# An attention and mixture kernel on one core: the transfers that stack q and k in another order, and the left queries' sums between the heads

## The chip, the cores and the metric

The kernel runs on one core of one Trainium2 chip. The metric is the device time of one execution in microseconds (us), taken as the median of several runs. The profile is one further execution, recorded by the hardware profiler.

## The reference

Inputs are fp32: q, k and v of 4 batches x 8 heads x 576 tokens x 64, and the weights of two feed-forward stages. What is computed:

```python
q_rot, k_rot = rotate(q), rotate(k)                  # rotary embedding
scores = (q_rot @ k_rot.T) / sqrt(64)
attn = exp(scores - rowmax);  attn = attn / (rowsum + 1e-9)
x = (attn @ v), heads side by side                   # 2304 x 512
x = (sigmoid(x @ w_gate) * (x @ w_val)) @ w_out      # hidden width 1536
h = x @ w_in                                         # hidden width 1024
solu = h * softmax(h);  ln = (solu - mean) / sqrt(var + 1e-6) * g
out = ln @ w_out2
```

## The kernel before, in words

The program has three stages one after the other: attention (about the first 300 us of the span), the gated stage with `gate_val` and `out_part`, and the last stage with the layer norm. The diff touches only attention, and of that only SyncE's transfers and the columns that the softmax's sums are written to.

**Pairs and steps.** Attention works through 16 pairs of heads (`pairs`). A pair has 9 groups of queries (`order`): four of 128 queries for head 0, one that holds the 64 left queries of both heads (tokens 512 to 575), four for head 1. A loop over `g` runs through 16 x 9 steps. At step g the kernel issues, in order: the row maximum of group g on VectorE (`row_max`, L376), the evacuations left over from the step before, the exponential on ScalarE with its row sums (`exps`, L381), the score matmuls of group g + 1 (`scores`, L369), and then what an agenda holds for this step (`advance`). The agenda is filled from the table `SLOTS`: for the pair that begins at step 9i, an entry `name=n` puts that work at step 9i + n. Within a step, entries of the kind REST run in the order in which the pairs registered them, a lower pair first.

**How q and k get to TensorE.** For a coming pair, GpSimd turns q and k (`turn`, at steps -16 and -15), TensorE transposes them in three parts (`qk_bank`, L303 and L306, at -11, -9 and -8), ScalarE and VectorE write a rounded part and a rest (L431, L434) into a tile of the pair, `st0`. As 4 blocks of 576 columns, its `flat` view holds: rounded k (0), rounded q (1), rest of k (2), rest of q (3); head 0 in partitions 0 to 63, head 1 in 64 to 127. `D` is 64, `P` is 128. For the scores the rounded part and the rest of one head must lie one above the other in 128 partitions, so `stack` (at -6) copies inside on-chip memory with five transfers from SyncE's queue. Three build the tile `st1` of head 1 (L315 to L317). Two then overwrite head 1's half of `st0` with head 0's parts (L318, L319); they must wait until the transfers that read the bytes to be overwritten have landed. The first scores of the pair, issued at step -1, read `st0`: the first matmul of them reads blocks 0 and 1 (written last by L318), the second reads blocks 1 and 2 (block 2 written by L319).

**The sums.** `exps` writes the sum of group n into one column of a 128 x 9 tile; `sum_at` puts the left queries' column last. `weigh` adds 1e-9 and takes the reciprocal (at 11), `weigh_t` transposes the nine columns on TensorE (13), `weigh_out` stores them as one run of 9 x 128 values in DRAM (14, L408), and `spread` (21, L416) broadcasts them back over partitions as the tile `wt` with four transfers: head 0 main, head 1 main, head 0 left, head 1 left. `scale_x` multiplies the output with it on GpSimd at step 24 (L426).

**SyncE's queue.** All these transfers are issued in program order from one queue, and one that waits holds up those behind it. Since 9(i - 3) + 21 = 9i - 6, the spread of pair i - 3 stands directly ahead of the stack of pair i. Behind it come, one step on, the loads of q and k of a later pair (`load_qk`, L211 and L215), `weigh_out` and the two `join` transfers (`um`, L487).

The tile framework puts in the waits itself, from the regions that each instruction reads and writes.

Of the kernel before, what the change touches and what calls it, by code (L numbers as in the profile page):

```python
# [20 lines left out]
def kernel(  # L21
# [21 lines left out]
    nc = tc.nc  # L43
    B, H, S, D = q.shape
# [3 lines left out]
    P = 128  # L48
    MAIN, LEFT, HALF = 512, 64, 288
# [155 lines left out]
    def load_qk(i, t=None):  # L205

        b, hp = pairs[i]
        hs = slice(2 * hp, 2 * hp + 2)
        raws[i] = t = raw_p.tile([P, 2, NSL, D], F32, tag="raw", name=f"raw{i}") if t is None else t
        for j, src in enumerate((k, q)):  # L210
            yield nc.sync.dma_start(  # L211
                out=t[:, :, 4 * j:4 * j + 4, :], in_=src[b, hs, 0:MAIN, :].rearrange("h (p r) d -> p h r d", r=4)
            )
        for j, src in enumerate((k, q)):
            yield nc.sync.dma_start(  # L215
                out=t[j * LEFT:(j + 1) * LEFT, :, 8, :], in_=src[b, hs, MAIN:S, :].rearrange("h t d -> t h d")
            )
# [90 lines left out]
            src = ps[:, 0:P].rearrange("p (a t) -> p a t", a=2)  # L308
        return [(h_out, l_out, src)]

    def stack(i):
        s0, s1 = stacks[i, 0].bitcast(F32), stacks[i, 1].bitcast(F32)
        flat = s0.rearrange("p a b s -> p (a b) s")
        dma = nc.sync.dma_start
        dma(out=s1[D:P], in_=flat[D:P, 0:3])  # L315
        dma(out=s1[0:D, 0:2], in_=flat[D:P, 2:4])
        dma(out=s1[0:D, 2], in_=flat[D:P, 0])  # L317
        dma(out=flat[D:P, 0:2], in_=flat[0:D, 2:4])  # L318
        dma(out=flat[D:P, 2], in_=flat[0:D, 0])  # L319

    def stack_first(h, step):

# [23 lines left out]

    order = [(0, 0), (0, 1), (0, 2), (0, 3), None, (1, 0), (1, 1), (1, 2), (1, 3)]
    NTL = len(order)
    sum_at = [0, 1, 2, 3, 8, 4, 5, 6, 7]
    e_tiles = {}  # L350
    sums = {}
    wts = {}
# [26 lines left out]
    def exps(i, n, ps, nm):  # L379
        e = e_p.tile([P, S], F32, tag="e", name=f"e{i}_{n}")  # L380
        nc.scalar.activation(  # L381
            out=e.rearrange("p (j c) -> p j c", j=2),
            in_=ps[:, :, :HALF],
            func=AF.Exp,
            bias=nm,
            accum_out=sums[i][:, sum_at[n]:sum_at[n] + 1],
        )
        e_tiles[i, n] = e

# [21 lines left out]
    def spread(i):  # L411
        d = wts[i]
        w = wt_p.tile([P, S], F32, tag="wt", name=f"wt{i}")
        for c0, n, at in ((0, MAIN, 0), (MAIN, LEFT, 2 * MAIN)):
            for h in range(2):
                nc.sync.dma_start(  # L416
                    out=w[h * D:(h + 1) * D, c0:c0 + n],
                    in_=d[at + h * n:at + (h + 1) * n].unsqueeze(0).to_broadcast([D, n]),
                )
        wts[i] = w  # L420

    def scale_x(i):
# [104 lines left out]
    FIRST, GROUP, ATTEND, REST = "first", "group", "attend", "rest"  # L527
    agenda = {}

    def at(g, kind, fn, *args):  # L530
        agenda.setdefault((g, kind), []).append((fn, args))


    SLOTS = dict(
        te=(1, 3, 4, 5, 6, 7, 8, 9, 11),
        corner=8,
        left=(6, 11),
        av=(((6, 2), (8, 9)), ((9, 4), (10, 9)), ((11, 2), (12, 6), (13, 9)), ((14, 9),)),
        join=(18, 19),
        add=(20, 24),  # L540
        weigh=11,
        weigh_t=13,
# [2 lines left out]
        scale=24,  # L545
        turn=(-16, -16, -15, -15),
        bank=(-11, -9, -8),
        stack=-6,
        split_v=-1,
        stack_left=0,  # L550
        load_qk=-23,
# [4 lines left out]
        sum_eng=0,  # L556
        uw=(1, 0, 0, 0),
        bank1=(1, 1, 1),
        stack1=3,
        first_b=(-1, -1, 2),  # L560
        turn1=(0, 0, 0, 0),
        split_v0=0,
# [29 lines left out]
    for i in range(NPR):  # L592
        g = i * NTL
        own = SLOTS_FIRST if i == 0 else SLOTS_LAST if i == NPR - 1 else SLOTS
        for n in range(NTL):
            at(g + own["te"][n], FIRST, transpose_e, i, n)
        at(g + own["corner"], GROUP, transpose_corner, i)
        for h in range(2):
            at(g + own["left"][h], GROUP, transpose_left, i, h)
            for j in range(2):  # L600
                m0 = 0
                for slot, m1 in own["av"][2 * h + j]:
                    at(g + slot, ATTEND, attend, i, h, j, m0, m1)
                    m0 = m1
            at(g + own["join"][h], REST, join, i, h)
            at(g + own["add"][h], REST, add, i, h)
        for name, fn in (
            ("weigh", weigh), ("weigh_t", weigh_t), ("weigh_out", weigh_out), ("spread", spread), ("scale", scale_x)
        ):
            at(g + own[name], REST, fn, i)  # L610

        if i > 1:
            at(max(0, g + SLOTS["load_qk"]), REST, lambda i: [None for _ in load_qk(i)], i)
            at(max(0, g + SLOTS["load_v"]), REST, load_v, i)
            for m, slot in enumerate(SLOTS["turn"]):
                at(max(0, g + slot), REST, turn, i, m)
        if i > 0:
            for part, slot in enumerate(SLOTS["bank"] if i > 1 else [b - NTL for b in SLOTS["bank1"]]):
                at(g + slot, GROUP, qk_bank, i, part)
            at(g + (SLOTS["stack"] if i > 1 else SLOTS["stack1"] - NTL), REST, stack, i)  # L620
            at(g + SLOTS["split_v"], REST, split_v, i)
            at(g + SLOTS["stack_left"], REST, stack_left, i)
    cur, late, moved = [], [], []
# [24 lines left out]
    for u in range(3):  # L648
        g = (W_PAIR + 2 * u) * NTL
# [36 lines left out]
    if True:  # L686
# [32 lines left out]
        for g in range(NPR * NTL):  # L719
            i, n = divmod(g, NTL)  # L720
            if g == (NPR - 1) * NTL:
                prep_ctx.close()
                xs_pool["p"] = x_ctx.enter_context(tc.tile_pool(name="xs", bufs=XS, side="right", reuse_waits="tile"))
            if g == 1:
                et = et_p.tile([P, 2, 2, 4, S], F32R, tag="et", name="et")
            nm = row_max(i, n, sc)
            if SLOTS["exp_pos"] == 0:
                exps(i, n, sc, nm)
            evacuate_h(cur)
            if SLOTS["exp_pos"] == 1:  # L730
                exps(i, n, sc, nm)
            evacuate_h(late)
            if SLOTS["exp_pos"] == 2:
                exps(i, n, sc, nm)
            evacuate_u()
            if SLOTS["exp_pos"] == 3:
                exps(i, n, sc, nm)
            evacuate_l()
            if g + 1 < NPR * NTL:
                sc = scores(*divmod(g + 1, NTL))  # L740
            advance(g)
# [381 lines left out]
```

## Time and profile before

| | |
|---|---|
| median of 3 runs | 967.11 us (964.16 to 969.16) |
| the profiled execution: its own time | 964.83 us |
| its span, first to last instruction | 963.1 us |
| mean granted TensorE clock | 0.995 of full |
| busy over the span: PE, PEld, DVE | 923.1 us, 801.5 us, 647.7 us |
| busy over the span: ACT, POOL | 501.7 us, 444.0 us |

PE is TensorE's matmuls, PEld its weight loads (which overlap matmuls), DVE is VectorE, ACT ScalarE, POOL GpSimd, SP SyncE. SPq is SyncE's queue of transfers. The shares over the whole span mix three stages with different limits; what attention is bound by has to be read from its own stretch.

### The profile page before, as it was taken

The numbers are of one execution on the slowest core, as the hardware profiler recorded it, in microseconds if no ns is written. First come the engines' busy times: TensorE is split into PE (matmuls) and PEld (weight loads), VectorE is DVE, ScalarE is ACT, GpSimd is POOL, SyncE is SP. The second block draws the span as 40 slices with busy tenths as digits, with TensorE's granted clock in tenths as the row PEclk, the third lists the DMA queues.
The fourth block names the chain that finished last, engine by engine and source line by source line (L and its number), as shares of the span: only waits on it lengthen the run. The fifth ranks groups of instructions, "written<-read, shape, count | busy, mean of one in ns | idle before, by whom it ended". The sixth has DMA issues, their size and how long they took to land.

```text
span 963.1 us, 14429 instructions
## 1 busy us (share of the span) xinstructions
PE 923.1 (96%) x5128; PEld 801.5 (83%) x5128; DVE 647.7 (67%) x1073; ACT 501.7 (52%) x994; POOL 444.0 (46%) x356
## 2 busy tenths in 40 slices
PE   4999999899999899999999999999999989999998
PEld 3889889899898688898788898788898768888886
DVE  7999989999888955346345355545456787666661
ACT  4888989898987323133111123112123576666662
POOL 5668879889845533344324344324343531111110
PEclk9999999999999999999999999999999999999999
DMA  3666677676754310103101012100112334334332
GB/s 108 141 169 165 152 191 180 160 188 159 160 141 122 104 66 22 44 23 94 38 22 44 23 45 88 44 22 22 44 46 71 103 64 90 66 72 93 66 77 44
DMA packets 92311, 86.10 MB, mean 89 GB/s; under 512 B 52608, under 2 KB 77456, under 8 KB 92240
## 3 DMA queue, kind: packets, MB, share of 16 engines
q1 hardware_dynamic: 92240, 85.19, 35.7%
q8 instruction: 40, 0.66, 0.3%
q14 instruction: 31, 0.25, 0.1%
HBM read 46.83 MB, written 4.79 MB: 54 GB/s over the span
## 4 chain that ended last, share of the span: by engine, by line
PE 63%; DVE 14%; DMA 10%; POOL 4%; issue 4%; ACT 2%; SPq 2%; DVEq 0%; POOLq 0%; ACTq 0%
DMA st<-st 9%; PE gv L680 9%; PE gv L681 9%; PE gv L679 9%; PE y L790 4%; PE y L789 4%; PE y L788 4%; PE po L977 3%; PE po L976 3%; PE po L978 3%; PE ph L881 3%; PE ph L882 3%; PE ph L883 3%; DVE nm L376 3%; DVE et L434 2%
## 5 line engine op out<-in xcount | busy, mean ns | idle before, releaser
L774 POOL TENSOR_TENSOR gs<-g,gs 128x512 fp32r<-128x512 f32 (+1 forms) x59 | 74.1, 1257 | 261.2 <-DVE gs L773 203.9
L769 ACT ACTIVATE sg<-gv 128x512 f32<-128x512 f32 (+1 forms) x60 | 33.3, 555 | 288.2 <-PE gv L681 288.2
L679 PE MATMUL gv<-xs,w 128*128 128x512 f32 (+1 forms) x480 | 177.4, 370 | 2.1 <-ACT w L137 2.1
L681 PE MATMUL gv<-xs,w 128*128 128x512 f32 (+1 forms) x480 | 177.5, 370 | 1.2 <-POOL w L138 1.2
L680 PE MATMUL gv<-xs,w 128*128 128x512 f32 (+1 forms) x480 | 177.4, 370 | 1.0 <-DVE xs L514 1.0
L771 DVE TENSOR_TENSOR g<-gv,sg 128x512 f32<-128x512 f32 (+1 forms) x60 | 38.2, 636 | 174.5 <-ACT sg L769 164.9
L381 ACT ACTIVATE e<-s,nm 128x576 f32<-128x576 f32 x144 | 107.3, 745 | 16.9 <-DVE nm L376 16.4
L369 PE MATMUL s<-st 128*128 128x288 f32 x512 | 102.8, 319 | 13.8 <-DMA st<-st 7.0
L376 DVE TENSOR_REDUCE nm<-s 128x1 f32<-128x576 f32 x144 | 107.2, 745 | 5.5 <-PE s L369 4.0
L681 PEld LDWEIGHTS gv<-xs,w 128*128 128x128 f32 x480 | 90.9, 189 | 17.3 <-POOL w L138 2.1
L680 PEld LDWEIGHTS gv<-xs,w 128*128 128x128 f32 x480 | 90.5, 189 | 17.5 <-DVE xs L514 2.7
L679 PEld LDWEIGHTS gv<-xs,w 128*128 128x128 f32 x480 | 90.5, 188 | 17.4 <-ACT w L137 2.5
L434 DVE TENSOR_TENSOR et<-te,et 128x512 fp32r<-128x512 f32 x144 | 98.3, 684 | 9.7 <-ACT et L431 8.5
L481 PE MATMUL av<-et,vs 128*128 128x288 f32 x512 | 99.9, 316 | 0.3 <-DVE uw L632 0.3
L369 PEld LDWEIGHTS s<-st 128*128 128x128 f32 x512 | 75.3, 193 | 23.2 <-DMA st<-st 6.3
L790 PE MATMUL y<-gs,w 128*128 128x512 f32 (+1 forms) x240 | 88.3, 368 | 0.0
L789 PE MATMUL y<-gs,w 128*128 128x512 f32 (+1 forms) x240 | 88.2, 368 | 0.0
L788 PE MATMUL y<-gs,w 128*128 128x512 f32 (+1 forms) x240 | 88.2, 367 | 0.0
L440 PE MATMUL te<-ident,e 128*128 128x128 f32 x576 | 87.0, 274 | 0.7 <-DVE et L434 0.7
L431 ACT CAST et<-te 128x512 fp32r<-128x512 f32 x144 | 84.2, 586 | 5.3 <-PE te L440 5.2
L481 PEld LDWEIGHTS av<-et,vs 128*128 128x128 f32 x512 | 73.0, 189 | 1.6 <-DVE uw L632 1.0
L440 PEld LDWEIGHTS te<-ident,e 128*128 128x128 f32 x576 | 71.1, 141 | 1.1 <-DVE et L434 0.9
(128 smaller groups left out, 1958.1 us busy)
## 6 DMA issues: line engine op xcount, KB each, us to landing
wraw<-in_moe_w_out_dram SPq DMA_DIRECT2D x20, 512.0 KB, 4.6
st<-st SPq DMA_DIRECT2D x30, 288.0 KB, 3.1
st<-st SPq DMA_DIRECT2D x15, 432.0 KB, 4.0
wraw<-in_moe_w_gate_dram SPq DMA_DIRECT2D x12, 512.0 KB, 4.0
wraw<-in_moe_w_val_dram SPq DMA_DIRECT2D x12, 512.0 KB, 4.5
um<-uw SPq DMA_DIRECT2D x32, 144.0 KB, 2.4
st<-st SPq DMA_DIRECT2D x30, 144.0 KB, 4.9
rawv<-in_v_dram SPq DMA_DIRECT2D x16, 256.0 KB
```

The source lines that it names most:

```text
L369: nc.tensor.matmul(ps[:, j, :HALF], w, x, start=m == 0, stop=m == len(mm) - 1)
L376: nc.vector.tensor_reduce(out=nm, in_=ps[:, :, :HALF], axis=AX.XY, op=ALU.max, negate=True)
L381: nc.scalar.activation(out=e.rearrange("p (j c) -> p j c", j=2), in_=ps[:, :, :HALF], func=AF.Exp, bias=nm, accum_out=sums[i][:, sum_at[n] ...
L434: nc.vector.tensor_sub(out=l_out, in0=ps, in1=h_out.bitcast(F32))
L440: nc.tensor.transpose(ps[:, r * P:(r + 1) * P], e[:, r * P:(r + 1) * P], ident)
L481: nc.tensor.matmul(av[:, :HALF], *mm[m], start=m == 0, stop=m == len(mm) - 1)
L679: nc.tensor.matmul(ps[:, :n], wh, x[:, 0, :n], start=kk == 0, stop=False)
L680: nc.tensor.matmul(ps[:, :n], wh, x[:, 1, :n], start=False, stop=False)
L681: nc.tensor.matmul(ps[:, :n], wl, x[:, 0, :n], start=False, stop=kk == KD - 1)
L788: nc.tensor.matmul(ys[m][:, :n], wh, g[:, 0, :n], start=first, stop=False)
L789: nc.tensor.matmul(ys[m][:, :n], wl, g[:, 0, :n], start=False, stop=False)
L790: nc.tensor.matmul(ys[m][:, :n], wh, g[:, 1, :n], start=False, stop=last)
```

## The change

`stack` is cut into two steps. Step 0 issues the four transfers that read head 1's half: the one that copied three blocks is cut into one of two blocks and one of one block, and the two that read the blocks which the first overwriting transfer needs now come first. Step 1 issues the two that overwrite. Both steps stand in the same slot (-6, and 3 for pair 1), one directly behind the other, so that six transfers stand where five stood. The sums go out in the order of the groups (the left queries' row between the heads, as row 4), and `spread` needs three transfers instead of four: head 0 whole, head 1 main, head 1 left.

```diff
-    def stack(i):
+    def stack(i, step):
+
         s0, s1 = stacks[i, 0].bitcast(F32), stacks[i, 1].bitcast(F32)
         flat = s0.rearrange("p a b s -> p (a b) s")
         dma = nc.sync.dma_start
-        dma(out=s1[D:P], in_=flat[D:P, 0:3])
-        dma(out=s1[0:D, 0:2], in_=flat[D:P, 2:4])
-        dma(out=s1[0:D, 2], in_=flat[D:P, 0])
-        dma(out=flat[D:P, 0:2], in_=flat[0:D, 2:4])
-        dma(out=flat[D:P, 2], in_=flat[0:D, 0])
+        if step == 0:
+            dma(out=s1[D:P, 0:2], in_=flat[D:P, 0:2])
+            dma(out=s1[0:D, 2], in_=flat[D:P, 0])
+            dma(out=s1[0:D, 0:2], in_=flat[D:P, 2:4])
+            dma(out=s1[D:P, 2], in_=flat[D:P, 2])
+        else:
+            dma(out=flat[D:P, 0:2], in_=flat[0:D, 2:4])
+            dma(out=flat[D:P, 2], in_=flat[0:D, 0])
...
-    sum_at = [0, 1, 2, 3, 8, 4, 5, 6, 7]
...
-            accum_out=sums[i][:, sum_at[n]:sum_at[n] + 1],
+            accum_out=sums[i][:, n:n + 1],
...
-        for c0, n, at in ((0, MAIN, 0), (MAIN, LEFT, 2 * MAIN)):
-            for h in range(2):
-                nc.sync.dma_start(
-                    out=w[h * D:(h + 1) * D, c0:c0 + n],
-                    in_=d[at + h * n:at + (h + 1) * n].unsqueeze(0).to_broadcast([D, n]),
-                )
+
+        for h, c0, n, at in ((0, 0, S, 0), (1, 0, MAIN, S + LEFT), (1, MAIN, LEFT, S)):
+            nc.sync.dma_start(
+                out=w[h * D:(h + 1) * D, c0:c0 + n], in_=d[at:at + n].unsqueeze(0).to_broadcast([D, n])
+            )
...
-        stack=-6,
+        stack=(-6, -6),
...
-        stack1=3,
+        stack1=(3, 3),
...
-            at(g + (SLOTS["stack"] if i > 1 else SLOTS["stack1"] - NTL), REST, stack, i)
+            for step, slot in enumerate(SLOTS["stack"] if i > 1 else [s - NTL for s in SLOTS["stack1"]]):
+                at(g + slot, REST, stack, i, step)
```

## Rows read from the trace of the kernel before

**Rows 1.** The page, busy us of the whole span, share and instructions.
```profile
PE 923.1 (96%) x5128; PEld 801.5 (83%) x5128; DVE 647.7 (67%) x1073; ACT 501.7 (52%) x994; POOL 444.0 (46%) x356
```
**Rows 2.** The page, the chain that ended last: shares of the span by line.
```profile
DMA st<-st 9%; PE gv L680 9%; PE gv L681 9%; PE gv L679 9%; PE y L790 4%; PE y L789 4%; PE y L788 4%; PE po L977 3%; PE po L976 3%; PE po L978 3%; PE ph L881 3%; PE ph L882 3%; PE ph L883 3%; DVE nm L376 3%; DVE et L434 2%
```
**Rows 3.** Windows of one pair each: stretch, length, busy us (x instructions) by engine.
```profile
core 0: us, PE busy (x) PEld busy (x) DVE busy (x) ACT busy (x) POOL busy (x), PEclk, DMA share, GB/s
50.60:68.19 17.59, 16.81 (x131) 16.11 (x132) 16.17 (x28) 15.84 (x38) 13.19 (x10) 1.00 0.65 156
68.19:85.55 17.36, 16.79 (x131) 16.06 (x131) 15.65 (x28) 15.39 (x38) 14.59 (x11) 1.00 0.71 169
85.55:102.52 16.97, 16.76 (x131) 16.11 (x131) 15.45 (x27) 15.10 (x37) 14.55 (x11) 1.00 0.70 166
102.52:120.84 18.32, 16.82 (x132) 16.11 (x132) 17.18 (x30) 16.80 (x41) 14.52 (x11) 1.00 0.66 155
...
156.53:174.74 18.21, 16.80 (x131) 16.08 (x131) 16.88 (x30) 17.22 (x42) 14.94 (x11) 1.00 0.76 192
...
192.30:210.11 17.81, 17.22 (x133) 16.09 (x131) 17.36 (x30) 17.09 (x42) 15.47 (x12) 1.00 0.79 189
...
sum 229.26, PE 218.38 PEld 208.67 DVE 211.92 ACT 204.97 POOL 186.77; mean PE 16.80 PEld 16.05 DVE 16.30 ACT 15.77 POOL 14.37
```
**Rows 4.** PE's waits, 30 to 300 us: total us, times, longest us.
```profile
PE s L369 <- DMA st<-st: 7.0, 16, 1.1
```
**Rows 5.** PE's timeline: start, us, instruction [idle before it and what ended it].
```profile
67.45 0.37 PE L369 MATMUL s<-st 128*128 128x288 f32 x1 [0.41 <-ACT et L431]
138.16 0.37 PE L369 MATMUL s<-st 128*128 128x288 f32 x1 [0.86 <-ACT st L431]
191.70 0.63 PE L303 MATMUL tq<-ident,turned 128*128 128x128 f32 x4 [1.03 <-DVE et L434]
209.43 0.37 PE L369 MATMUL s<-st 128*128 128x288 f32 x1 [0.26 <-ACT et L431]
227.09 0.63 PE L303 MATMUL tq<-ident,turned 128*128 128x128 f32 x4 [1.05 <-DVE et L434]
```
**Rows 6.** SyncE's queue over one stack: start and duration of each issue.
```profile
161.57 2.46 SPq L416 DMA_DIRECT2D wt<-d  x4
164.13 0.54 SPq L315 DMA_DIRECT2D st<-st  x1
164.72 0.59 SPq L316 DMA_DIRECT2D st<-st  x1
165.35 1.60 SPq L317 DMA_DIRECT2D st<-st  x1
170.77 0.46 SPq L318 DMA_DIRECT2D st<-st  x1
171.33 0.54 SPq L319 DMA_DIRECT2D st<-st  x1
```
**Rows 7.** The chain over the same stack: start, us, what.
```profile
165.35 5.40 DMA st<-st
...
171.33 3.37 DMA st<-st
...
174.74 0.67 PE s L369 x3
```
**Rows 8.** Line L318, its 14 transfers: issue to landing.
```profile
DMA to landing us min/median/max: 3.1/3.1/3.1
```
**Rows 9.** Line L317, its 14 transfers: issue to landing.
```profile
DMA to landing us min/median/max: 4.9/5.6/6.2
```
**Rows 10.** The page, transfers: count, KB each, median us to landing.
```profile
st<-st SPq DMA_DIRECT2D x15, 432.0 KB, 4.0
...
um<-uw SPq DMA_DIRECT2D x32, 144.0 KB, 2.4
```
**Rows 11.** DVE's waits, 30 to 300 us.
```profile
DVE et L434 <- ACT et L431: 6.1, 22, 0.5
```

## The prediction

> **What bounds the kernel now.** I first read the page. TensorE's matmuls fill 96% of the span [rows 1], so time comes back only where PE stands idle, or where its work shrinks; the change takes no work from PE. The chain that ended last gives 9% of the span to one kind of transfer, `st<-st` [rows 2], which is `stack`. That share is no price: it says that the chain runs through those transfers, not how long anyone waited for them. So I cut attention into windows of one pair, each ending where the second of a pair's score matmuls could go [rows 3]. In 13 pairs (229.26 us) PE is idle 229.26 - 218.38 = 10.9 us. The reader is to see what is left of a pair when PE's idle time is taken off: 17.59 - 0.78, 17.36 - 0.57, 16.97 - 0.21, 18.32 - 1.50, 18.21 - 1.41 leave 16.81, 16.79, 16.76, 16.82 and 16.80. The idle time differs by a factor of seven and the rest is constant. PE makes up nothing of what it lost, so a stall of PE here costs its full length.
>
> Then who causes the stalls. The list of PE's waits names the stack's landing 16 times, 7.0 us [rows 4]. Three more waits of a pair's first score matmul, 0.41 + 0.86 + 0.26 = 1.53 us, are put down to ScalarE [rows 5]; the matmul behind each of them waits for the stack again, and I count these to the stack too: 8.5 us in 11 pairs, 0.78 us for each pair that waits. Nearly all of the rest is two waits of 1.03 and 1.05 us for the transposes of the next pair (L303) [rows 5], which the change doesn't touch. Pair 1 stacks five steps before its first scores are issued and has nothing to gain.
>
> Last, SyncE's queue over one stack [rows 6]. The three transfers that build `st1` are issued at 164.13, 164.72 and 165.35; L318, which overwrites, goes only at 170.77, right where the third landed (165.35 + 5.40 [rows 7]). L319 follows at 171.33 and lands 3.37 later, at 174.70; PE goes on at 174.74 [rows 7]. So the path is: first issue, 6.6 us until the third has landed, 0.6 us to L319's issue, 3.4 us to its landing: 10.6 us. From 170.75 until L318 starts nothing of the stack is in flight.
>
> **The change, part by part.**
>
> *The overwriting transfers.* Now the first of them needs only the first two reads, 288 and 144 KB, which is just the size and order of L318 and L319. That pair lands 3.1 [rows 8] and 0.56 + 3.37 = 3.9 us after the first issue [rows 6, 7]. So the first overwriting transfer goes 3.9 us after the stack's start instead of 6.6, while the other two reads are still in flight, and stands behind their bytes. The bytes of the four reads are the same 864 KB, so I let them land where the three did, 6.6 us after the start. Behind them 144 KB more take 0.83 us (L318 lands at 170.77 + 3.1 = 173.87, L319 at 174.70), so 288 KB take about 1.6 and the first overwriting transfer lands at 8.2, against 6.6 + 3.1 = 9.7 before: 1.5 us earlier. The second waits for the other two reads, goes at 6.7, and lands behind the first at 8.2 + 0.8 = 9.0, or at the 2.4 us that 144 KB take alone [rows 10], 6.7 + 2.4 = 9.1; against 10.6 that is 1.5 earlier. I take 1.4. Bounds: nothing, if the first overwriting transfer is made to wait for all four reads; 2.7 us if the stream's bytes cost it nothing (6.6 - 3.9). Against the first bound speaks that L319 doesn't wait for L318, though both write one tile, and that a pair's first matmul goes before L319 has landed [rows 5, 7]: waits go by region.
>
> *One more issue.* The cut transfer adds an issue of 0.46 to 1.60 us on SyncE [rows 6]; the third in a row takes 1.60 and may hand that wait to the fourth. I take 0.6 and price it at nothing, because SyncE waits from about 3 to 3.9 and up to 6.6 us anyway; if that cover were gone it would cost 0.6 us of the 1.4. How late three reads land varies from 4.9 to 6.2 us [rows 9], and moves both orders alike.
>
> *Spread.* Four issues take 2.46 us and the stack's first issue stands 0.1 us behind them [rows 6]; three take 0.6 less. Where the stack's source is written earlier than that, its start moves by up to 0.6 us; where it waits for VectorE, by nothing. I take 0.2 for a mean. The sum on SyncE is neutral past the stack (six for five, three for four), and what stands behind (loads of q and k, `weigh_out`, the joins) is free about as much sooner as the start moves. `scale_x` reads `wt` three steps later, so the larger single transfer stays hidden; exposed it would cost some tenths of a microsecond on GpSimd, which is busy 14.4 of 17.6 us [rows 3].
>
> *The sums' columns.* The same activations write to other columns: nothing, either way. `weigh` waits for all nine as before.
>
> *What the landing is worth.* Landing 1.4 to 1.6 us sooner covers waits of 0.21 to 1.50 us [rows 3], so at most 8.5 us go. What is late next is VectorE: it is busy 17.18, 16.88 and 17.36 us in three pairs that hold weight decoding [rows 3], and it loses 6.1 us in some 15 pairs, 0.4 a pair, waiting for ScalarE's half of an evacuation [rows 11]. With that these pairs can't go below 17.6, 17.3 and 17.8, which leaves 0.7, 0.9 and 0 us to gain in place of 1.5, 1.4 and 0.6: 1.9 us given up. Shorter pairs also bring the first scores some 0.3 us closer to the stack; in the three longest waits that leaves about 0.3 us each, 0.9 in all. Sum: 8.5 - 1.9 - 0.9 = 5.7, and I take 6 us.
>
> One rule speaks against the cut: the Trainium skill, "DMA: Bandwidth & Descriptors", section "Rules for kernel authors", says to coalesce many small transfers into one large one, and that transfers to separate partition halves run one after the other. By it, the two pieces of the cut transfer cost more than the whole. The row says that a 144 KB transfer behind one of 288 KB adds 0.83 us, the rate of its bytes and no more [rows 6, 7, 8]; by the row the cut costs nothing in the stream. What the rule would make of the time is the second rival.
>
> A second rule concerns the stalls: "Trainium Kernel Development and Optimization" of the Trainium skill, section "Best Practices", has distance from the limit judged by weight loads rather than by matmul busy time. PEld is busy 16.05 us a pair and PE 16.80 [rows 3]; by the rule PE could catch up 0.75 us a pair, and then most stalls would already be absorbed and the sum would be near nil. The constant rest of 16.8 us is the measurement against it.
>
> **The rivals.**
>
> 1. *The stalls turn into other waits.* VectorE is busy 16.3 us of 17.6 on the mean, ScalarE 15.8 [rows 3], each in strict order; freed of the stack, PE may wait for row maxima, evacuations or the transposes of the next pair. For it: the 1.03 and 1.05 us waits for L303 are there already [rows 5]. Against it: the pair that waited only 0.21 us took 16.97 us, so the other engines can do such a pair; but that pair held no decoding. If only the pairs without decoding gain (about 0.78 + 0.57 + 0.21 and 0.4 for the pair before them, some 2 us) the time is 965. The case in which the framework holds the first overwriting transfer for all four reads comes out alike: 0.2 us a pair from the spread, 11 x 0.2 = 2 us. Both: no change that a measurement tells.
> 2. *The extra transfer costs a transfer's own time (slower).* If the fourth read ran after the third instead of in its stream, it would land 2.4 us later [rows 10], and the second overwriting transfer, which needs it, with it: 2.4 - 1.4 = 1.0 us later than before, on 11 pairs that already wait, 11 us: 978. It decides from an added 1.4 us on. The 0.83 us of [rows 6 to 8] speaks against it. The Trainium skill's rule on small transfers, above, points this way.
> 3. *All of it comes off.* No engine takes the place of the stack: 8.5 us, 958, with the spread's share helping in the longest pairs. For it speaks the constant rest of a pair; against it VectorE's 17.2 and 17.4 us.
>
> **How the numbers follow.** The forecast (a part of the stalls goes, 4 to 7.5 us) has 0.6, the first rival 0.2, the second 0.05, the third 0.15. The sum is made against the profiled execution's own 964.83 us (its span and 1.7 us around it): 964.8 - 6 = 959. That execution lies 2.3 us under the median of the runs, 967.1; from the median it would be 961. The mean of the four executions shown is 966.3, so I say 960.5. The range must take in the full 8.5 us from the profiled time, 956, and nearly the whole first rival counted from the median, 965.5. A measurement of this kernel tells about 0.5% from no change, 4.8 us. Most of the forecast and all of the third rival lie beyond that, allowing for the runs' own spread: faster 0.63; within it the first rival and the small end of the forecast: 0.31; slower, the second rival: 0.06.
>
> **What would show it.** In the profile after: the first overwriting issue about 4 us after the stack's first, before the third and fourth reads have landed; the second at 6.6 to 6.8, landing near 9.1 instead of 10.6. PE's wait for `st<-st` falls from 7.0 us to 2 or less, pairs without decoding come to 16.8 to 17.0 us, pairs with decoding stay at 17.3 to 17.8, and the chain leaves `st<-st` for VectorE. PE's busy time doesn't move. The prediction is wrong if the overwriting issue still stands 6.6 us behind the first, if PE's idle total of 10.9 us stays and only changes its names, or if the four reads land more than 1 us later than the three.

## The result and the profile after

The changed kernel takes 956.5 us (median of 4 runs, 956.12 to 958.3) against 968.13 us (4 runs, 964.16 to 970.14): a ratio of 0.9896, 95% interval 0.986 to 0.9932. The forecast was 960.5 us with a range from 956.0 to 965.5, and a chance of 0.63 for faster by over 0.5%. The direction and the place were right, the gain is larger than forecast: the time lies 0.5 us above the lower end of the range. The two profiled executions stand at 964.83 and 956.12 us, 8.7 us apart.

Line numbers of the changed kernel are a few higher than before: L317 to L320 are the four reads of the stack, L322 and L323 the two transfers that overwrite, L372 the scores, L419 the spread.

The page of the kernel after, engines and the chain that ended last:

```profile
PE 922.3 (97%) x5128; PEld 800.5 (84%) x5128; DVE 648.3 (68%) x1073; ACT 499.0 (52%) x994; POOL 443.5 (46%) x356
PE 75%; DVE 12%; POOL 5%; issue 3%; DMA 3%; ACT 2%; SPq 0%; DVEq 0%; POOLq 0%; ACTq 0%
```

PE does the same work as in [rows 1], and `st<-st`, which led [rows 2] with 9%, is no longer among the lines that the page lists for the chain. Before, the chain by engine was:

```profile
PE 63%; DVE 14%; DMA 10%; POOL 4%; issue 4%; ACT 2%; SPq 2%; DVEq 0%; POOLq 0%; ACTq 0%
```

What the transfers gave up went to PE, from 63 to 75%. The forecast that VectorE would take their place did not hold: its share fell from 14 to 12%.

SyncE's queue over one stack of the kernel after (start, duration of the issue), which answers to [rows 6]:

```profile
157.54 0.48 SPq L317 DMA_DIRECT2D st<-st  x1
158.06 0.59 SPq L318 DMA_DIRECT2D st<-st  x1
158.76 0.79 SPq L319 DMA_DIRECT2D st<-st  x1
159.59 0.76 SPq L320 DMA_DIRECT2D st<-st  x1
161.50 0.46 SPq L322 DMA_DIRECT2D st<-st  x1
164.51 0.46 SPq L323 DMA_DIRECT2D st<-st  x1
```

The first overwriting issue stands 161.50 - 157.54 = 4.0 us behind the stack's first (6.6 before), the second 7.0. Over the 14 stacks it is 3.9 to 4.2 us for the first (6.1 to 7.4 before) and 6.3 to 7.9 for the second (6.6 to 8.0 before). The four issues take no longer than the old three: the third, 1.60 us in [rows 6], takes 0.79, and the fourth 0.76. Issue to landing of L323, its 14 transfers:

```profile
DMA to landing us min/median/max: 2.3/2.3/2.3
```

So the stack ends 7.0 + 2.3 = 9.3 us after it begins, where it took 10.6: the last transfer goes a little sooner and lands sooner, 2.3 us after its issue where it took 3.3 to 3.4. PE's waits from 30 us to the end of attention in the kernel after (total us, times, longest), which answer to [rows 4, 5]:

```profile
PE tq L303 <- DVE et L436: 2.6, 2, 1.3
...
PE s L372 <- DMA st<-st: 0.2, 1, 0.2
```

The 8.5 us for the stack are 0.2. To see what a pair takes, both kernels are cut at the scores of the left queries, which stand in each pair once. Before (columns as in [rows 3]; three of 14 pairs and the sum):

```profile
109.85:128.16 18.31, 16.81 (x134) 16.10 (x132) 15.94 (x28) 15.61 (x38) 15.03 (x12) 1.00 0.78 181
...
146.22:163.85 17.63, 16.89 (x134) 16.09 (x132) 16.78 (x30) 15.69 (x38) 15.38 (x12) 1.00 0.76 186
...
182.06:199.91 17.85, 16.82 (x133) 16.03 (x132) 17.60 (x30) 15.65 (x38) 15.82 (x13) 1.00 0.78 188
...
sum 246.37, PE 234.76 PEld 224.10 DVE 226.59 ACT 220.23 POOL 196.62; mean PE 16.77 PEld 16.01 DVE 16.18 ACT 15.73 POOL 14.04
```

The same pairs after:

```profile
107.70:124.41 16.71, 16.71 (x134) 16.05 (x132) 15.66 (x28) 15.34 (x38) 14.56 (x12) 1.00 0.79 193
...
141.26:158.73 17.47, 17.08 (x134) 16.06 (x132) 17.28 (x30) 15.50 (x38) 15.39 (x12) 1.00 0.82 194
...
175.58:194.12 18.54, 17.09 (x134) 16.05 (x132) 18.35 (x30) 15.55 (x38) 16.51 (x13) 1.00 0.72 181
...
sum 238.92, PE 234.64 PEld 223.45 DVE 227.74 ACT 217.69 POOL 196.78; mean PE 16.76 PEld 15.96 DVE 16.27 ACT 15.55 POOL 14.06
```

PE's busy time is the same to 0.1 us; its idle time falls from 11.6 to 4.3 us. Eleven of the 14 pairs are now 16.6 to 16.9 us long, with PE idle for at most 0.2 us in ten of them; in the last it waits twice for ScalarE's exponential, 0.8 us in all, as it did before. Three are not: the 17.47 and 18.54 us shown and another of 18.53, with VectorE busy for 99% of them; the two of 18.5 us are 0.7 us longer than they were. The 14 pairs together give 246.37 - 238.92 = 7.45 us. The gated stage begins 8.9 us earlier; the first of its matmuls before and after:

```profile
300.10 0.39 PE L679 MATMUL gv<-xs,w 128*128 128x512 f32 x1
```

```profile
291.21 0.39 PE L682 MATMUL gv<-xs,w 128*128 128x512 f32 x1
```

The remaining 1.43 us come in the last pair: from the left queries' scores to that matmul it took 300.10 - 287.10 = 13.0 us and now takes 291.21 - 279.64 = 11.57. From there to the end of the span it is 663.0 us before and 663.1 after: nothing came or went after attention.

### The profile page after: what moved, and what is told of

It is laid out like the page before. It is cut to its first block, busy times and chain, and to the rows that moved or that the text cites. A ratio compares the mean times of both kernels' runs of the same rounds, so it can differ in the third digit from the quotient of the medians.

```text
span 954.3 us, 14445 instructions
## 1 busy us (share of the span) xinstructions
PE 922.3 (97%) x5128; PEld 800.5 (84%) x5128; DVE 648.3 (68%) x1073; ACT 499.0 (52%) x994; POOL 443.5 (46%) x356
## 4 chain that ended last, share of the span: by engine, by line
PE 75%; DVE 12%; POOL 5%; issue 3%; DMA 3%; ACT 2%; SPq 0%; DVEq 0%; POOLq 0%; ACTq 0%
PE gv L683 9%; PE gv L684 9%; PE gv L682 8%; PE s L372 6%; PE av L483 5%; PE y L793 4%; PE y L792 4%; PE y L791 4%; PE te L442 4%; PE po L981 3%; PE po L980 3%; PE po L979 3%; PE ph L884 3%; PE ph L885 3%; PE ph L886 3%
## 5 line engine op out<-in xcount | busy, mean ns | idle before, releaser
L384 ACT ACTIVATE e<-s,nm 128x576 f32<-128x576 f32 x144 | 107.2, 744 | 18.4 <-DVE nm L379 17.6
L372 PE MATMUL s<-st 128*128 128x288 f32 x512 | 100.7, 319 | 5.6 <-ACT e L384 2.6
L682 PEld LDWEIGHTS gv<-xs,w 128*128 128x128 f32 x480 | 90.4, 188 | 17.3 <-ACT w L137 2.4
L372 PEld LDWEIGHTS s<-st 128*128 128x128 f32 x512 | 74.7, 193 | 12.5 <-ACT e L384 7.2
```

Of the source, the lines that this page charges most:

```text
L372: nc.tensor.matmul(ps[:, j, :HALF], w, x, start=m == 0, stop=m == len(mm) - 1)
L384: nc.scalar.activation(out=e.rearrange("p (j c) -> p j c", j=2), in_=ps[:, :, :HALF], func=AF.Exp, bias=nm, accum_out=sums[i][:, n:n + 1],)
L682: nc.tensor.matmul(ps[:, :n], wh, x[:, 0, :n], start=kk == 0, stop=False)
```

## The experiments

What the experiments were to tell apart: that the gain comes from the *order* (the first overwriting transfer waits for two reads only, and starts while the others are in flight); from the *queue* (one spread issue fewer ahead of the stack); or from the *cut* (the 432 KB transfer). Then what a stall of PE costs, and what is left.

| kernel | median, us | ratio to before, 95% interval | gated stage begins, us | PE waits for `st<-st` by name, us |
|---|---|---|---|---|
| e1_sums_only | 963.35 | 0.9973 (0.9957 to 0.9988) | 297.81 | 6.8 |
| e2_stack_only | 956.08 | 0.991 (0.9893 to 0.9927) | 292.25 | 1.3 |
| e3_order_no_cut | 956.06 | 0.991 (0.9894 to 0.9925) | 291.35 | 0.3 |
| e4_cut_needed_last | 962.43 | 0.9957 (0.9939 to 0.9974) | 295.98 | 3.9 |
| e10_after_again | 956.82 | 0.9895 (0.9876 to 0.9914) | 290.83 | none |
| e9_swap_only | 955.51 | 0.9884 (0.9866 to 0.9902) | 291.49 | 1.5 |
| e6_stack_late | 956.03 | 0.9892 (0.9871 to 0.9912) | 290.81 | none |
| e8_decode_spread | 957.23 | 0.9905 (0.9889 to 0.9922) | 292.78 | none |
| e11_overwrite_behind_loads | 994.46 | 1.0308 (1.0288 to 1.0328) | 325.38 | 19.8 |
| e12_no_integer_steps | 951.33 | 0.9857 (0.984 to 0.9875) | 286.40 | none |

Each group was compared with the kernel before on its own chip: the first four with 966.54 us, the next four with 966.65, the last two with 964.96.

**e1_sums_only.** The kernel before with `sum_at` left out and the new spread.

```diff
-    sum_at = [0, 1, 2, 3, 8, 4, 5, 6, 7]
...
-        for c0, n, at in ((0, MAIN, 0), (MAIN, LEFT, 2 * MAIN)):
...
+        for h, c0, n, at in ((0, 0, S, 0), (1, 0, MAIN, S + LEFT), (1, MAIN, LEFT, S)):
```

> The old five stacking transfers in their old order, with the new sums and the spread of three transfers. Order theory (the gain comes from the first overwriting transfer waiting for two reads instead of all): the overwriting issue still stands 6.6 us behind the stack's first, the stack starts up to 0.6 us sooner in the pairs where SyncE was the limit, PE still waits 5 to 6.5 us in all for the stack; 1 to 2.5 us faster than before (ratio 0.9975 to 0.999). Rival, queue theory (the missing spread issue ahead of the stack does it): 6 us faster or more, PE's wait for the stack under 2 us.

Its queue, and PE's wait:

```profile
126.90 0.48 SPq L315 DMA_DIRECT2D st<-st  x1
...
134.21 0.46 SPq L318 DMA_DIRECT2D st<-st  x1
```

```profile
PE s L368 <- DMA st<-st: 6.8, 17, 1.0
```

L318 still stands 7.3 us behind the stack's first issue here (6.1 to 7.3 over the 14 stacks, as before), and PE waits for the stack by name nearly as long as before, 0.3 us more than expected. 0.27%, 2.6 us faster: just beyond the upper end of what the order theory allowed, and far from the 6 us of the queue theory.

**e2_stack_only.** The changed kernel with the old `sum_at` and the old spread of four.

> The new stack (six transfers, the two that overwrite last, the needed reads first), with the old columns of the sums and the spread of four. Order theory: overwriting issue about 4 us behind the first, PE's wait for the stack under 1.5 us, 7 to 9 us faster than before (ratio 0.990 to 0.993). Queue theory: less than half of the change's 10 us, and PE still waits 4 us or more.

PE's wait for the stack is 1.3 us and the time 956.08, 0.9% faster: as the order theory has it. The changed kernel is not measurably faster than this (956.5, and 956.82 again): with the order in place, the spread's missing issue adds nothing that can be measured, though alone it gave 2.6 us. The two parts shorten the same stalls.

**e3_order_no_cut.** The changed kernel with five transfers.

```diff
-            dma(out=s1[D:P, 0:2], in_=flat[D:P, 0:2])
+            dma(out=s1[D:P], in_=flat[D:P, 0:3])
             dma(out=s1[0:D, 2], in_=flat[D:P, 0])
             dma(out=s1[0:D, 0:2], in_=flat[D:P, 2:4])
-            dma(out=s1[D:P, 2], in_=flat[D:P, 2])
```

> The changed kernel with the cut undone: five transfers, the three-block read of 432 KB first, then the 144 KB one, then the 288 KB one, then the two that overwrite. Order theory: the first overwriting issue comes at 4.8 to 5 us (576 KB instead of 432 KB ahead of it), its landing is still set by the stream of bytes, so at most 1 us in all is lost against the change: 9 to 11 us faster than before (ratio 0.989 to 0.991). Rival, cut theory (the large 432 KB transfer is what clogs the queue, its third issue takes 1.6 us): less than half of the gain is left, ratio 0.995 or more.

```profile
124.04 0.48 SPq L317 DMA_DIRECT2D st<-st  x1
...
125.20 1.65 SPq L319 DMA_DIRECT2D st<-st  x1
129.00 0.46 SPq L321 DMA_DIRECT2D st<-st  x1
```

The third issue takes 1.65 us as before and the overwriting one comes at 5.0 us (4.7 to 6.1 over the 14 stacks, beyond the 5 expected in five of them); the time is 956.06. The second overwriting issue, which the stack ends with, comes no later than in the changed kernel, 6.1 to 7.1 us behind the first against 6.3 to 7.9. The cut is worth nothing here, and the long third issue costs nothing.

**e4_cut_needed_last.** The changed kernel, the same six transfers, the two that the first overwriting transfer needs in third and fourth place.

> The changed kernel with the same six transfers, but the two reads that the first overwriting transfer needs go third and fourth. Order theory: the first overwriting issue falls back to 6.6 to 7.2 us behind the stack's first, PE waits 5 us or more for the stack, only what the spread gives is left: 0 to 2.5 us faster than before (ratio 0.9975 to 1.0). Cut theory: 5 us faster or more. If an extra transfer costs a transfer's own time, slower than before by 5 us or more.

```profile
126.50 0.48 SPq L317 DMA_DIRECT2D st<-st  x1
...
132.75 0.46 SPq L322 DMA_DIRECT2D st<-st  x1
```

```profile
PE s L372 <- DMA st<-st: 3.9, 11, 0.9
...
PE s L372 <- ACT st L433: 0.9, 1, 0.9
```

The overwriting issue falls back to 6.25 us (a little less than the 6.6 expected) and the stalls return, 3.9 us by name and 0.9 put down to ScalarE. It is 0.43% faster than before, somewhat more than the 0.25% expected at most; its interval and that of e1 overlap. The extra transfer doesn't make it slower.

**e9_swap_only.** The kernel before with two lines swapped and nothing else.

```diff
         dma(out=s1[D:P], in_=flat[D:P, 0:3])
-        dma(out=s1[0:D, 0:2], in_=flat[D:P, 2:4])
         dma(out=s1[0:D, 2], in_=flat[D:P, 0])
+        dma(out=s1[0:D, 0:2], in_=flat[D:P, 2:4])
```

> The kernel before with only its second and third stacking transfers swapped, so that the first overwriting transfer needs the first two of three reads; no cut, old sums, old spread of four. Order theory: the first overwriting issue comes 4.8 to 5.5 us behind the stack's first instead of 6.6, PE's wait for the stack falls under 2 us, 8 to 10 us faster than before (ratio 0.9895 to 0.992). Rival, parts theory (the swap needs the cut or the spared spread issue beside it, since each shortens the path by some tenths): 6 us or less, PE still waits 3 us or more.

 

> The changed kernel once more, beside the next three on one chip: ratio 0.988 to 0.991 to the kernel before, 956 to 957 us. It is what the others are compared with.

955.51 us beside 956.82 of the changed kernel on the same chip: the swap alone gives the whole gain. PE still waits 1.5 us for the stack by name: the overwriting issue comes 4.9 us behind the first early in attention (45.15 - 40.28), but 5.5 to 6.3 us in five stacks further on, where 5.5 was expected at most. In the five pairs there that costs some tenths (86.8 us, from 107.32 to 194.16; 86.4 in the changed kernel, from 107.70 to 194.12), less than the measurement tells.

**e6_stack_late.** The changed kernel with `stack=(-5, -5)`.

> The changed kernel with both stack steps one step later (-5 instead of -6), so that the landing comes about 1.8 us later. Stalls cost their full length: PE waits for the stack in 11 pairs or more, 0.5 to 1 us each, and the span grows by that total within a fifth, 6 to 12 us above the changed kernel. Rival, catch-up (PE makes stalls good, as its weight loads are busy 0.75 us less a pair than its matmuls): the span grows by less than half of what PE waits.

The expectation fell at its premise. 956.03 us, no wait for the stack; the first stacking issue after the spread at 121.45 comes at 123.38, and in the changed kernel's own second profile it comes at 123.43 after a spread at 121.51. Between steps -6 and -5 nothing else goes into SyncE's queue, and SyncE's queue goes by its own order, not by the steps: here the slot moved nothing. e11 moves it past other transfers.

**e11_overwrite_behind_loads.** The changed kernel with `stack=(-6, -4)`.

> The changed kernel with the two overwriting transfers two steps later in the program (stack=(-6, -4)), so that the four loads of q and k and the store of the sums stand ahead of them in SyncE's queue; here the landing really moves, to about 12 us behind the stack's first issue, where PE wants it at 10.4. Stalls cost their full length: PE waits 8 to 22 us in all for the stack, and attention grows by that total within a fifth. Rival, catch-up: attention grows by less than half of what PE waits.

```profile
121.64 0.48 SPq L317 DMA_DIRECT2D st<-st  x1
...
129.28 0.51 SPq L322 DMA_DIRECT2D st<-st  x1
```

The overwriting transfer goes at 7.6 us, behind the loads, and the second lands at about 11.7, close to the 12 expected. PE waits 19.8 us for the stack by name and 4.6 us more at the same matmuls, 24.4 in all; attention grows by 325.38 - 291.21 = 34.2 us, 40% more than the waits, where the expectation allowed a fifth. So stalls are not made good, but that each costs just its length failed as well: most of the long ones here cost more. The windows of one such stall say why (columns as in [rows 3]):

```profile
49.50:53.10 3.60, 0.09 (x1) 0.00 (x0) 1.98 (x4) 2.36 (x5) 1.17 (x1) 1.00 0.78 184
53.10:54.30 1.20, 1.17 (x5) 1.04 (x6) 0.00 (x0) 0.00 (x0) 1.03 (x5) 0.73 0.60 165
54.30:55.50 1.20, 1.20 (x8) 1.20 (x7) 0.76 (x1) 0.26 (x1) 1.20 (x1) 0.50 0.78 219
...
56.70:59.00 2.30, 2.30 (x19) 2.30 (x18) 2.01 (x4) 1.58 (x4) 2.22 (x2) 0.92 0.00 0
```

PE stood idle for 3.5 us; half a microsecond after it goes on, the granted clock falls to 0.50, the lower of the two levels (1.2 GHz), until about 57 us, and the four score matmuls at 53.13 take 1.22 us where the next but one take 0.77. Over the 14 pairs PE's busy time is 246.3 us instead of 234.6 (e11's sum of windows against that of the kernel after): 11.7 us, on top of 22.6 us more idle time.

The length of a stall alone doesn't say what follows it. Of the seven stalls of more than 1 us in e11, four are followed by some 3.4 us at 0.50 (those that end at 53.13, 113.11, 152.47 and 192.81, 3.55, 1.24, 2.33 and 3.79 us long; the second has 0.43 us more of waiting right behind it). Two are followed by more: after 3.45 and 2.05 us of waiting (to 92.46 and 252.02) the clock stays at 0.50 for 6.8 us, from before the stall has ended. And after 2.30 us (to 232.20) it stays at 1.00. The window behind the stall of 1.24 us, and the pair with the one of 2.30:

```profile
115.00:117.00 2.00, 2.00 (x11) 1.93 (x10) 0.81 (x3) 0.82 (x3) 2.00 (x4) 0.52 0.65 197
...
220.04:240.39 20.35, 17.19 (x133) 16.12 (x132) 17.30 (x29) 16.58 (x40) 16.66 (x13) 1.00 0.59 142
```

In the kernel before, whose longest wait of PE in the pairs is 1.15 us (to 120.11), the granted clock was 1.00 in all of them.

**e8_decode_spread.** The changed kernel with other slots for the decoding of the first weights.

```diff
-        decode=(3, 5, 13, 15, 23, 29),
+        decode=(3, 5, 7, 16, 23, 30),
```

> The changed kernel with the last four steps of the weight decoding in other slots (7, 16, 23, 30 instead of 13, 15, 23, 29): VectorE's two integer steps with two inputs fall in different pairs, where GpSimd is idle, and GpSimd's step falls behind the turning. VectorE theory (what is left of PE's idle time, 17.5, 18.5 and 18.5 us in three pairs against 16.7 to 16.9 in the others, is VectorE's load there): these pairs come to 17.3 us or less, the waits for L303 fall from 2.8 us to under 1.5, 2 to 4 us faster than the changed kernel. Rival (it is GpSimd's lateness with the turned q and k, not VectorE): VectorE's busy time in these pairs stays above 17.5 us and less than 1 us is gained, or the waits move to other pairs.

A miss: 957.23 us, no gain. The waits for L303 vanish and others come in their place:

```profile
PE tl L454 <- DVE et L436: 2.7, 6, 0.7
```

Six pairs that hold a step of the decoding are now long, where three were; two of them, and the pair behind them without one:

```profile
195.48:213.53 18.05, 17.31 (x133) 16.05 (x132) 17.61 (x30) 16.34 (x40) 14.74 (x12) 1.00 0.64 160
213.53:231.10 17.57, 17.31 (x133) 16.07 (x132) 16.53 (x29) 15.33 (x38) 16.09 (x13) 1.00 0.69 162
231.10:247.80 16.70, 16.70 (x133) 16.01 (x132) 15.58 (x28) 15.85 (x39) 14.53 (x12) 1.00 0.70 169
```

The second is long with VectorE busy for only 94% and one integer step in it: a long instruction seems to cost its time wherever it stands ahead of the row maxima and evacuations that PE waits for. The waits for L303 are gone, so GpSimd's lateness is not what lengthens these pairs; whether VectorE is, this placement alone doesn't show.

**e12_no_integer_steps.** The changed kernel; `w_decode` skips VectorE's two steps with two inputs for the first hidden block, whose weights are then only signs.

```diff
+        if i == 0:
+            yield
+            yield
+        else:
             yield nc.vector.scalar_tensor_tensor(
...
             yield nc.vector.scalar_tensor_tensor(
```

> The changed kernel without VectorE's two two-input integer steps (L123, L126) for the first weight, six instructions in attention of 0.7 to 1.7 us each; the first hidden block's weights are then only signs. VectorE theory (what is left of PE's idle time is these steps): the pairs of 17.5, 18.5 and 18.5 us fall to 17.0 or less, PE's waits for L303 to under 1 us, 3.5 to 4.5 us faster than the changed kernel, 952 to 953. Rival (GpSimd late with the turned q and k, because its step of the decoding stands between): waits for L303 stay above 2 us and less than 1.5 us is gained.

951.33 us, 0.9857 of the kernel before on its chip (the changed kernel had 0.9896, and 0.9895 again), and the gated stage begins at 286.40, 4.8 us sooner than in the changed kernel's profile. The first and the last of the three pairs that were long (the third is 16.71 us):

```profile
140.94:157.63 16.69, 16.69 (x134) 16.01 (x132) 15.64 (x28) 15.34 (x38) 14.54 (x12) 1.00 0.81 194
...
208.04:224.73 16.69, 16.69 (x134) 16.04 (x132) 15.65 (x28) 15.31 (x38) 15.73 (x13) 1.00 0.70 170
```

They are PE's length now, with as many of GpSimd's instructions as before (12 and 13) and its step of the decoding still in place; those instructions take 0.8 us less (14.54 and 15.73 us for 15.39 and 16.50), so this run alone doesn't part VectorE from GpSimd. The changed kernel's own trace does. At the first of the two waits for L303, PE goes on when VectorE's evacuation ends, and that stands directly behind L126 and a row maximum (VectorE's and PE's timelines of the kernel after):

```profile
185.08 0.68 DVE L436 TENSOR_TENSOR et<-te,et 128x512 fp32r<-128x512 f32 x1
```

```profile
185.90 0.63 PE L303 MATMUL tq<-ident,turned 128*128 128x128 f32 x4 [1.31 <-DVE et L436]
```

GpSimd's last instruction on the turned q and k had ended at 183.94. Of PE's 4.3 us of idle time in the 14 pairs 1.0 is left in e12 (234.12 us, PE busy 233.16), most of it the last pair's waits for ScalarE; the rest went with these six instructions.

## Why the prediction was right, and where its sizes were off

**The bound.** Right. That PE makes up nothing of a stall was read from the constant rest of a pair, and the pairs after are that rest: 16.7 us, where 16.8 was read. That a stall costs just its length holds for stalls like those of the kernel before; in e11 most longer ones cost more. The rule of the Trainium skill on weight loads ("Trainium Kernel Development and Optimization", section "Best Practices") would have left PE 0.75 us a pair to catch up; neither the changed kernel nor e11 shows any of it.

**The overwriting transfers.** Right, and by e2, e3 and e9 the whole of the gain. Forecast: issues at 3.9 and 6.7 us, the end at 9.1; measured 4.0, 7.0 and 9.3 in the stack shown. The first overwriting transfer, forecast to land at 8.2, lands 3.7 us after its issue, at 7.7. The region-wise waits that it needed are there: the first overwriting issue stands ahead of the landing of the fourth read, which takes 4.9 us and more.

**The extra issue.** Right that it costs nothing (e3 against the changed kernel). The Trainium skill's advice to coalesce ("DMA: Bandwidth & Descriptors", section "Rules for kernel authors") does not show against the cut at these sizes, 144 and 288 KB: e3, which has the larger transfer, takes 956.06 us and the changed kernel 956.5 and 956.8. The second rival is out.

**Spread.** Taken at 0.2 us a pair. Alone (e1) it gives 2.6 us in all. In its profile the gated stage begins 2.3 us sooner; 1.5 of them lie in the 14 pairs, 0.1 a pair, and 0.7 in the stretch behind them, which is told below. Beside the order it gives nothing that shows: the stalls that it shortens are gone.

**What the landing is worth.** The mechanism held, the sizes didn't. The term of 8.5 us for the stalls was right (8.3 went). Of the 1.9 us put down to VectorE, the pair with 18.32 us in [rows 3], which I held to 17.6, fell to 16.7, and the one with 18.21, held to 17.3, to 16.85. The 17.18 us of VectorE in the first were the window's doing: it holds 30 of VectorE's instructions, and cut at the left queries' scores the pairs there have 28 and 15.9 us. In its place two pairs that had waited for L303 grew by 0.69 and 0.66 us. In both, VectorE's step L123 took 0.68 us before and takes 1.38 now, which is as much (the line of VectorE in the first of them before; the one after stands in the last section):

```profile
L123 DVE SCALAR_TENSOR_TENSOR val<-mag,val 128x512 int32<-128x512 int32 x1 | 0.7, 683 | 0.0
```

VectorE took back 1.35 us there, and the other twelve pairs gave 8.80. The 0.9 us for shorter pairs did not come: 0.2 us of wait is left. So the pairs gave 7.45 us where the sum had 5.7.

**A term that I had at nothing.** I priced SyncE being free sooner behind the stack as neutral. In the last pair it is worth 1.43 us. The `join` stands behind the stack and two loads of weights there; in the kernel before its landing is late, GpSimd waits for it, and VectorE's reciprocal waits for GpSimd's add in `weigh`. GpSimd's and VectorE's timelines before:

```profile
286.27 1.42 POOL L493 TENSOR_TENSOR x_sb<-uw,um 64x576 f32<-64x576 f32 x1 [2.23 <-DMA um<-uw]
287.77 0.25 POOL L393 TENSOR_SCALAR sum<-sum 128x9 f32<-128x9 f32 x1
```

```profile
288.06 0.22 DVE L394 RECIPROCAL sum<-sum 128x9 f32<-128x9 f32 x1 [1.49 <-POOL sum L393]
```

After, the joins are issued 9.4 us ahead of the left queries' scores instead of 7.7 (270.22 against 279.64; 279.40 against 287.10), and neither wait is there. The other kernels agree: where VectorE waits 0.8 us (e1) and 0.7 us (e4) for that add, the last stretch takes 12.3 and 12.2 us; in e2, e3, e9 and e12, where it doesn't wait, 11.6. No run moved the join by itself.

**The two medians.** With 7.45 + 1.43 = 8.9 us the profiles are accounted for. The medians lie 11.6 us apart, and 9.8 beside e10. The profiled execution of the kernel before is among its shorter ones (964.83 us; its runs spread from 964 to 970), and the lower end of the range was counted from it: that the measured time still lies inside, though the medians fell by more than the 8.5 us of the third rival, owes something to that choice. Part of the spread goes with the mean granted clock: beside e10 the kernel before takes 968.1 to 968.6 us in three runs at 0.992 and 965.3 to 966.9 in three at 0.996, the changed kernel 956.8 to 958.1 and 955.0 to 955.2. At equal clock they lie 10 to 12 us apart there; what the 1 to 3 us beyond the 8.9 are is open, as there is one trace of the kernel before.

**The rivals.** The first (the stalls turn into other waits) happened in two pairs of 14; the third (all of it comes off) is nearest to what was measured, with 8.9 us for its 8.5, but for another reason: VectorE did take some back, and the join gave as much again. That the two cancel is chance.

## What to carry to other kernels

Where a transfer overwrites what others read, put the reads that it needs at the head of the queue, so that it is issued while the rest is still in flight; here two swapped lines gave 1%. On an engine that makes up no time, price a stall at its full length at least, then look on the queue for what else was waiting behind the blocked transfer. A slot in the program's schedule moved a transfer here only where something else stood between the old place and the new in its own queue (e6 against e11).

## What the runs showed of the hardware

A stall of 3.55 us cost PE 1.6 us more than its length (18.19 us busy in that pair of e11 for 16.62 in the kernel after), because the granted clock stood at 0.50 for some 3.4 us after it; one of 2.05 us was followed by 6.8 us at 0.50, one of 2.30 us by none (e11).

And VectorE's integer steps took up to 1.74 us in attention (L126) and 1.38 (L123); in the last pair, with GpSimd idle as it began, L123 took 0.69. VectorE's and GpSimd's timelines after:

```profile
178.66 1.38 DVE L123 SCALAR_TENSOR_TENSOR val<-mag,val 128x512 int32<-128x512 int32 x1
182.75 1.74 DVE L126 SCALAR_TENSOR_TENSOR val<-wraw,val 128x512 int32<-128x512 int32 x1
281.35 0.69 DVE L123 SCALAR_TENSOR_TENSOR val<-mag,val 128x512 int32<-128x512 int32 x1
```

```profile
176.82 2.67 POOL L245 TENSOR_TENSOR raw<-raw,rope_sb 128x1152 f32<-128x1152 f32 x1
...
181.15 2.79 POOL L253 TENSOR_TENSOR turned<-raw,other 128x576 f32<-128x576 f32 x2
```

Both slow ones in attention end some 0.55 us after an instruction of GpSimd that was under way when they began (179.49 and 183.94). "SBUF — State Buffer" of the Trainium skill, section "SBUF: two separate sides", has VectorE with two inputs from on-chip memory and GpSimd take one port pair by turns, for a whole instruction; the trace agrees with it, and no run here tried it by itself. The same L126 in the pair of 17.47 us began at 148.42, just ahead of an instruction of GpSimd (148.45), and took 0.68 us, while GpSimd's took 1.93 for its usual 1.42.
